# Transposes of queries, keys and attention output by DMA instead of by TensorE products, in an attention + MLP kernel

## The chip, the cores and the metric

One core of a Trainium2 chip. Times are device microseconds (us) of one execution. "Faster" and "slower" mean by over 2%. Executions that lie over 1.5% above the fastest of the same kernel count as slow; every ratio below is from fast executions alone. "Half clock" means that the profile records TensorE's granted clock at half of full speed. A bank is a piece of PSUM that holds one result.

## The reference, cut to what matters

Cosine attention for 8 batches of 12 heads, 448 positions and 64 elements; its output, with the heads side by side, is the input of a two-layer MLP.

```python
q_n = q / (norm(q, axis=-1) + 1e-6)            # q, k, v: (8, 12, 448, 64), fp32
k_n = k / (norm(k, axis=-1) + 1e-6)
attn = softmax(q_n @ k_n.T / tau)               # tau = 0.1
x = (attn @ v) with heads side by side          # (3584, 768)
h = x @ w_in                                    # (768, 2048)
out = (h * clip(h + 3, 0, 6) / 6) @ w_out       # (2048, 768)
```

## The kernel before

The kernel works on 48 pairs of heads. The first 18 pairs are run from a hand-written plan, in which every token is one step; pairs 18 to 47 are run by a loop. In iteration i the loop computes the scores and probabilities of pair i, finishes pair i - 1, prepares pair i + 2, and puts "units" of the MLP of the batch before (`UU`) between these, so that TensorE has work while other engines do theirs. Queries and keys are loaded with positions on partitions, but the score product reads them with the 64 elements of a head on partitions (`64*128 64x448` in the profile). So each normalised tile `nrm` (128 partitions, 7 slots, 2 heads of 64) is transposed by seven products with the identity, and the result is copied out of PSUM:

```python
def products(j, part):                      # "TM": one tile of queries or keys, in two parts
    t0, n = ((0, 4), (4, 3))[part]
    z, key = bank_of(None, readers(j, t0, n))
    for t in range(n):
        o = z[:, t * 128 : (t + 1) * 128]
        nc.tensor.matmul(o, nrm[:, slots(j)[t0 + t], :, :], ident[:, :], start=True, stop=True)

def copy_k(i, e="v", part=None):            # "CK": six slots of 64 keys, PSUM fp32 -> SBUF bf16
    ...
    copy(e, kz[i % 2][:, c0 + 64 * (a - odd) : c0 + 64 * (b - odd)], z[:, a - t0 : b - t0, x, :])

def copy_k3(i, e="v"):                      # "CS": the seventh slot, each half on its own partitions
    ...
    for g in range(2):
        p = slice(64 * g, 64 * g + 64)
        copy(e, kz[i % 2][p, c : c + SR], z[p, t : t + 1, x, :])      # 64 partitions x 64 elements

# the loop
for i in range(FIRST, NP):
    for g in range(3): do("SC", i, g)       # scores, then exponentials, then probabilities x values
    ...
    do("FI", i - 1); do("SC", i, 3); do("EX", i, 3)
    for part in range(2):
        prepare(("TM", i + 2, part))        # queries in even iterations, keys in odd ones
        if even:  prepare(("CQ", i + 2, "v", part), ("CQ", i + 3, "v", part))
        else:     ...                       # CK and CS of pairs i + 1 and i + 2
        if part == 0: do("UU", 1)
    prepare(("SQ", i + 5, "p", 0, 7))       # "p": GpSimd
    do("UU", n - 1)
    do("BK", i - 1); do("CX", i - 1, ...)   # attention output: 4 products, one copy from PSUM
    if not even: prepare(("NO", (i + 3) // 2))
    do("UU", n_u - n)
    prepare(("NM", i + 3, "p"), ("VC", i + 2, "p"), ("RE", i + 5), ("LQ", i + 7))
    if not even: prepare(("LV", (i + 5) // 2))
    do("VA", i, 0)
```

GpSimd computes squares (`SQ`), normalises (`NM`) and casts values (`VC`); VectorE has the copies, the MLP's product `gT` and the sums.

## Time and profile before

| | before |
|---|---|
| time, 3 runs | 456.58 us (451.35 to 458.17) |
| span of the profiled run | 452.1 us |
| TensorE busy | 432.4 us (96%), 3,891 matmuls |
| VectorE, ScalarE, GpSimd busy | 62%, 62%, 38% |
| load and store queue, share of 16 DMA engines | 37.9% |
| chain of work that ended last | 87% of the span on TensorE |

Busy shares are of the span. What counts is the last row: after the loads of the start, TensorE is never without work (idle for 0.04 us after 80 us), so the time is TensorE's list of work. The lines that show it are in the prediction. Two more groups matter later, the small key copies, which read PSUM in the kernel before, and the score products. In the groups, the columns are count, busy us, mean ns of one, and the idle time before them:

```profile
L317 DVE CAST kz<-M 64x64 bf16<-64x64 f32 x40 | 8.7, 217 | 0.5 <-PE M L306 0.2
L395 PE MATMUL M<-qT,kz 64*128 64x448 bf16 (+1 forms) x193 | 41.8, 353 | 1.1 <-DVE kz L359 0.5
```

### The profile page before, as it was taken

The page shows a single profiled execution, that of the slowest core. Times are in us where ns is not written, and L with a number is a line of the kernel's source. Part 1 is how long each engine was busy: PE and PEld are TensorE (multiplying, and loading weights), DVE is VectorE, ACT ScalarE, POOL GpSimd, SP SyncE. Part 2 cuts the span into 40 slices and gives each one's busy share as a digit, 9 for nine tenths or more (in the row PEclk, how much of TensorE's full clock was granted, in tenths as well). Part 3 has the DMA queues.
Part 4 walks back from the last instruction along what each step waited for, and adds up shares of the span by engine and source line. Part 5 has one row for each costly group of instructions (what it writes and reads, how often), then busy time and mean ns, then how long its engine had stood idle before and what let it go on. Part 6 is the DMA issues. An engine that isn't in the chain of part 4 may idle for free.

```text
span 452.1 us, 9918 instructions
## 1 busy us (share of the span) xinstructions
PE 432.4 (96%) x3891; PEld 259.8 (57%) x3891; DVE 279.1 (62%) x603; ACT 279.7 (62%) x625; POOL 172.0 (38%) x149
## 2 busy tenths in 40 slices
PE   4879799999999999999999999999999999999996
PEld 1446455556665666666666666666666665655563
DVE  6888688678566675576776675566776552304400
ACT  5769799986676755576576575567577565214410
POOL 4869479603007361542652551633641400000000
PEclk9669999999999999999999999999999999999999
DMA  7999999912252443435343444425432011121032
GB/s 218 276 226 263 252 233 215 233 24 79 68 146 78 125 136 85 123 79 145 107 128 95 110 106 131 122 60 137 128 83 65 19 32 40 36 70 36 0 72 70
DMA packets 39695, 52.55 MB, mean 116 GB/s; under 512 B 4320, under 2 KB 38112, under 8 KB 39648
## 3 DMA queue, kind: packets, MB, share of 16 engines
q1 hardware_dynamic: 35536, 45.07, 37.9%
q0 software_dynamic: 3712, 6.29, 7.8%
q8 instruction: 30, 0.49, 0.5%
q10 hardware_dynamic: 400, 0.56, 0.4%
q14 instruction: 17, 0.14, 0.1%
HBM read 47.19 MB, written 11.01 MB: 129 GB/s over the span
## 4 chain that ended last, share of the span: by engine, by line
PE 87%; DMA 7%; issue 2%; POOL 1%; SPq 1%; ACT 1%; DVE 0%; POOLq 0%; ACTq 0%
PE M L493 23%; PE M L527 21%; PE PV L437 10%; PE Z L493 7%; PE Y L527 6%; PE M L395 5%; PE Z L527 5%; DMA raw<-in_k_dram 3%; DMA w_in_sb<-in_moe_w_in_dram 3%; PE Y L493 2%; PE Z L395 2%; PE M L306 2%; PE M L474 1%; PE Y L306 1%; PE Y L395 1%
## 5 line engine op out<-in xcount | busy, mean ns | idle before, releaser
L527 PEld LDWEIGHTS <-gT 128*128 128x128 bf16 x896 | 86.8, 98 | 57.6 <-issue 0.2
L493 PE MATMUL M<-xT,w_in_sb 128*128 128x448 bf16 x546 | 115.3, 352 | 0.0
L250 POOL TENSOR_TENSOR nrm<-raw,r 128x896 bf16<-128x896 f32 (+1 forms) x44 | 74.6, 1697 | 102.4 <-ACT r L238 102.3
L412 ACT ACTIVATE at<-M 128x448 bf16<-128x448 f32 x193 | 93.7, 564 | 29.8 <-PE M L395 20.0
L493 PEld LDWEIGHTS <-w_in_sb 128*128 128x128 bf16 x768 | 70.5, 98 | 57.0 <-issue 4.5
L527 PE MATMUL M<-w_out_sb,gT 128*128 128x384 bf16 x592 | 101.0, 326 | 0.0
L207 POOL TENSOR_TENSOR sq<-raw 128x896 f32<-128x896 f32 (+7 forms) x46 | 67.0, 1458 | 70.2 <-DMA raw<-in_k_dram 28.9
L508 DVE SCALAR_TENSOR_TENSOR gT<-u,M 128x448 bf16<-128x448 bf16 x91 | 56.2, 620 | 32.4 <-ACT u L502 31.2
L502 ACT ACTIVATE u<-M,half_bias 128x448 bf16<-128x448 f32 x91 | 58.8, 649 | 23.5 <-PE M L493 22.8
L437 PEld LDWEIGHTS <-at 128*128 128x128 bf16 x1344 | 54.1, 99 | 24.9 <-issue 19.0
L437 PE MATMUL PV<-vx,at 128*128 128x65 bf16 (+1 forms) x1344 | 65.5, 200 | 0.0
L219 DVE TENSOR_REDUCE n<-sq 128x14 f32<-128x896 f32 (+1 forms) x50 | 51.8, 1040 | 2.4 <-POOL sq L207 1.5
L395 PE MATMUL M<-qT,kz 64*128 64x448 bf16 (+1 forms) x193 | 41.8, 353 | 1.1 <-DVE kz L359 0.5
L412 ACT ACTIVATE at<-Z 128x448 bf16<-128x448 f32 x56 | 31.6, 564 | 13.2 <-PE M L395 13.1
L544 DVE COPY o<-M 128x384 f32<-128x384 f32 x19 | 10.6, 557 | 42.5 <-PE M L527 42.5
L493 PE MATMUL Z<-xT,w_in_sb 128*128 128x448 bf16 x162 | 35.1, 352 | 0.0
L453 DVE TENSOR_TENSOR on<-PV,rc 128x512 bf16<-128x512 f32 x48 | 33.2, 692 | 1.7
L452 DVE RECIPROCAL rc<-PV 128x8 f32<-128x8 f32 x48 | 9.9, 206 | 37.8 <-PE PV L437 37.8
L542 ACT COPY o<-M 128x384 f32<-128x384 f32 x17 | 8.1, 478 | 38.6 <-PE M L527 38.6
L527 PE MATMUL Y<-w_out_sb,gT 128*128 128x384 bf16 x176 | 30.4, 326 | 0.0
L263 POOL CAST vx<-vr 128x512 bf16<-128x512 f32 x43 | 26.2, 614 | 10.9 <-DMA vr<-in_v_dram 10.9
L412 ACT ACTIVATE at<-Y 128x448 bf16<-128x448 f32 x45 | 25.3, 563 | 0.1
(91 smaller groups left out, 432.1 us busy)
## 6 DMA issues: line engine op xcount, KB each, us to landing
vr<-in_v_dram SPq DMA_DIRECT2D x96, 128.0 KB, 4.0
out_dram<-o SPq DMA_DIRECT2D x111, 96.0 KB, 2.2
raw<-in_q_dram SPq DMA_DIRECT2D x23, 448.0 KB, 5.3
raw<-in_k_dram SPq DMA_DIRECT2D x23, 448.0 KB, 4.0
w_in_sb<-in_moe_w_in_dram POOLq DMA_DIRECT2D x4, 768.0 KB, 12.5
w_out_sb<-in_moe_w_out_dram POOLq DMA_DIRECT2D x4, 768.0 KB, 11.1
raw<-in_q_dram SPq DMA_DIRECT2D x4, 112.0 KB, 3.4
raw<-in_k_dram ACTq DMA_DIRECT2D x4, 112.0 KB, 3.7
```

The costliest lines, as they stand in the source:

```text
L207: engines[e].tensor_tensor(out=o, in0=i, in1=i, op=ALU.mult)
L219: nc.vector.tensor_reduce(out=n2s[d % 2][:, j % 2, c], in_=sq[:, :, :, :].rearrange("p g c d -> p (g c) d")[:, c, :], axis=AX.X, op=ALU.add,)
L250: engines[e].tensor_tensor(out=nrm[:, :, g, :].rearrange("p c g d -> p g c d"), in0=raw_of[j][:, g, :, :], in1=rs[d % 2][3][:, j % 2, :] . ...
L263: engines[e].tensor_copy(out=vx[i % NVX][:, :, 0:D].rearrange("p (g c) d -> p g c d", g=2), in_=bass.AP(tensor=(t := vr[i // 2 % NV][:, i ...
L395: nc.tensor.matmul(o, kt[rows, c0 : c0 + 128], qt[rows, :], start=True, stop=True)
L412: nc.scalar.activation(out=o, in_=x, func=AF.Exp, scale=inv_tau)
L437: nc.tensor.matmul(o, at[:, n, q_cols(i // HP, j)], mv, start=(name == "A0" and j % 2 == 0), stop=last, skip_group_check=True,)
L453: nc.vector.tensor_tensor(out=on[:, :, :, :].rearrange("p (b j) h d -> p b (j h) d", b=2), in0=pv4[:, :, :, 0:D], in1=rc[:, :, :].to_broad ...
L493: nc.tensor.matmul(ps[:, 0:S], w_in_sb[:, cc, fc * 128 : (fc + 1) * 128], x[:, cc, :], start=(cc == 0), stop=(cc == CC - 1),)
L502: nc.scalar.activation(out=u[:, :], in_=ps[:, 0:S], func=AF.Relu, bias=half_bias[:, :], scale=1.0 / 6.0)
L508: nc.vector.scalar_tensor_tensor(out=g[:, fc, c0 : c0 + S], in0=u[:, :], scalar=1.0, in1=ps[:, 0:S], op0=ALU.min, op1=ALU.mult,)
L527: nc.tensor.matmul(ps[:, 0:MH], lhs, w_out_sb[:, fc, m * MH : (m + 1) * MH], start=(fc == 0), stop=(fc == FCN - 1),)
```

## The change

Its intent is to take the transposes off TensorE. From tile 14 on, `nrm` is transposed by one DMA, SBUF to SBUF (`XD`), and from pair 12 on the attention output too (`XB`), both on the sync queue. The score product reads queries straight from the transposed tile `tT`, so the query copies go. The key copies now read `tT` in SBUF. Positions keep their natural slot order. In the loop, the keys' copies move behind the second MLP unit.

```diff
+    def crossbar(j):
+        ...
+        nc.sync.dma_start_transpose(
+            out=tT[j % 4][:, :, :, :].rearrange("p c n e -> p c (n e)"),
+            in_=nrm[:, :, :, :].rearrange("p c g d -> p (c g d)"),
+        )
+    def back_crossbar(i):
+        ...
+        nc.sync.dma_start_transpose(
+            out=xT[b % 2][:, hp, :].rearrange("p (j n) -> p j n", j=4),
+            in_=on[:, :, :, :].rearrange("p j h d -> p (j h d)"),
+        )
     def copy_k(i, e="v"):
         ...
+        f = bass.AP(tensor=f.tensor, offset=f.offset, ap=[f.ap[0], [128, 3], [512, 2], [1, 64]])
+        nc.vector.tensor_copy(out=kz[i % 2][:, 0:KM].rearrange("p (j h e) -> p j h e", j=3, h=2), in_=f)
     def copy_k3(i, e="v"):
         ...
         for g in range(2):
             ...
             copy(e, kz[i % 2][p, c : c + SR], z[p, t : t + 1, x, :])   # z is now tT, in SBUF
     def scores(...):
         ...
+        kt, qt = kz[i % 2], tT[jq % 4][:, :, i % 2, :] if jq >= XJ else qT[i % 4]
     # the loop
-        for part in range(2):
-            prepare(("TM", i + 2, part))
-            ...
-            if part == 0:
-                do("UU", 1)
+        do("XB", i - 1)
+        prepare(("XD", i + 2))
+        do("UU", 1)
         prepare(("SQ", i + 5, "p", 0, 7))
         do("UU", n - 1)
-        do("BK", i - 1)
-        do("CX", i - 1, "a" if i % HP == 0 else "v")
+        if not even:
+            prepare(("CK", i + 1), ("CS", i + 1), ("CK", i + 2), ("CS", i + 2))
...
-    NV, NR = 3, 8
+    NV, NR = 3, 7
```

Cut: the same replacement in the plan (`TM`, `CQ`, `BK`, `CX` become `XD`, `XB`), slot order, fills of the pads, one buffer of `u` fewer (3, not 4), and the order of two units at a batch's start.

## The prediction

> **What bounds the kernel now.** I read first the page of the profile (busy shares, the slices, the chain that ended last), then the view of windows, then the timeline of one steady iteration, engine by engine. The slices:
>
> ```profile
> PE   4879799999999999999999999999999999999996
> ...
> POOL 4869479603007361542652551633641400000000
> PEclk9669999999999999999999999999999999999999
> DMA  7999999912252443435343444425432011121032
> ...
> PE 87%; DMA 7%; issue 2%; POOL 1%; SPq 1%; ACT 1%; DVE 0%; POOLq 0%; ACTq 0%
> ```
>
> The kernel has two stages. Until about 80 us the DMA rows are full (loads of queries, keys, values and weights) and TensorE is not. From 80 us on TensorE is busy in every slice, at the full granted clock, and the chain that ended last runs along it for 87% of the span. DMA is at 0.1 to 0.5 there. A busy TensorE need not be at its peak, so I look at one steady iteration in the timeline of TensorE (start, length, what):
>
> ```profile
> 242.44 0.35 PE L395 MATMUL M<-qT,kz 128*128 128x448 bf16 x1
> 242.63 0.39 PE L306 MATMUL Y<-ident,nrm 128*128 128x128 bf16 x4
> 242.90 1.29 PE L493 MATMUL Z<-xT,w_in_sb 128*128 128x448 bf16 x6
> 244.03 0.33 PE L306 MATMUL M<-ident,nrm 128*128 128x128 bf16 x3
> 244.19 1.30 PE L493 MATMUL M<-xT,w_in_sb 128*128 128x448 bf16 x6
> 245.33 0.36 PE L474 MATMUL M<-ident,on 128*128 128x128 bf16 x4
> 245.53 1.30 PE L493 MATMUL M<-xT,w_in_sb 128*128 128x448 bf16 x6
> 246.66 2.76 PE L527 MATMUL Y<-w_out_sb,gT 128*128 128x384 bf16 x16
> 249.26 0.41 PE L437 MATMUL PV<-vx,at 128*128 128x65 bf16 x8
> ```
>
> Each block starts as soon as the one before allows: six products of the first MLP matmul take 1.13 us (188 ns each), sixteen of the second 2.60 us (163 ns). There is no gap to win; only work can be taken off. The iteration lasts some 8.6 us, and in the windows of 20 us from 160 to 260 us VectorE is busy 12 to 14 us, ScalarE 11 to 13, GpSimd 8 to 11: none is near being the bound.
>
> [...] what such a product costs in a full pipeline: one record lasts 219 ns, while the next matmul starts 50 to 60 ns after it. I count by starts.[...] Nothing in the kernel before shows a DMA transpose[...].[...] in this iteration two stores issued at 241.4 and 242.0 move their 1,536-byte packets until about 244, and then the 1,792-byte packets of the load issued at 242.6 follow, to about 246.
>
> **The change, part by part.** *Taken from TensorE.* From the instruction lists: all 238 products of line 306 (queries and keys, 34 tiles of two heads by 7) and 144 of the 176 of line 474 (attention output, 36 head pairs by 4). From the timeline, per pair: 242.63 to 242.90 is 0.27 us, 244.03 to 244.19 0.16, 245.33 to 245.53 0.20. That is 34 x 0.43 + 36 x 0.20 = 21.8 us. Summed over the whole trace from each product's start to the next matmul's, line 306 costs 238 x 58.5 ns = 13.9 us and the removed part of line 474 144 x 50.4 ns = 7.3 us: 21.2 us, all after 80 us, all on the path. I use 21.2.
>
> *Taken from VectorE and ScalarE.* 61 query copies (30 of 349 ns, 31 of 415), 29 copies of attention output (618 ns) and 25 small copies on ScalarE go; the key copies read bf16 in SBUF, not fp32 in PSUM. That is over 40 us of VectorE and some 9 of ScalarE, beside the path: worth nothing by itself. Three PSUM banks fewer per pair are taken from the ring of six; TensorE did not wait for banks, so nothing either.
>
> *Added.* 34 DMA transposes of 128x896 bf16 (229 KB) and 36 of 128x512 (131 KB), 12.5 MB, all on the sync queue, which executes in order and already has loads and stores.[...] In 360 us that adds 35 GB/s to rows that are under half used: bandwidth is no bound. Latency is the question, in three places.
>
> (a) Odd iterations, 14 in the loop. There the keys' transpose is issued right behind the attention output's, and VectorE's key copies stand after the second MLP unit, ahead of the third unit's product. In the trace the last probability product of the pair before ends near 242.6, normalising on VectorE ends at 243.57, and the sync queue is free by 243.2. So the output's transpose goes out at 243.6. Issue: 0.6 us, what a load's issue takes[...] (a store takes 2.2 us from issue to landing, 0.55 of it issue)[...]. When is it needed? Without the removed products, the next scores start at 242.6 + 3 x 1.13 + 2.6 + 0.5 = 249.1, the third pair of them at 249.5, in the bank that the third unit's product has to free; that product (0.62) stands behind the key copies (about 1 us): the transpose has to land by 247.9. The estimate is 0.3 to 0.8 us late[...]. I take 0.35 us x 14 = 5 us.
>
> (b) Batch boundaries, five in the loop. The last pair's output is needed by the first unit of the next batch. The change puts a second-matmul unit ahead of it: two carried units and that one, 2.26 + 2.6 + 0.2 = 5.1 us after the last probability product. But the sync queue has a query load and four value loads ahead. The boundary near 288 us, where that product ends at 288.4:
>
> ```profile
> 288.50 0.59 SPq L176 DMA_DIRECT2D raw<-in_q_dram  x1
> 289.20 2.64 SPq L191 DMA_DIRECT2D vr<-in_v_dram  x4
> ```
>
> So the output's transpose is issued from 291.85, 3.4 us after the product, with 960 KB ahead in the rings;[...] some 0.8 us late. 5 x 0.8 = 4 us.
>
> (c) The planned part before pair 18, and the start: one raw buffer fewer (7, not 8) makes loads wait for one normalisation more, 1 to 2 us each while DMA is the bound; 8 small fills more on GpSimd. I take 1 us.
>
> Sum: 21.2 - 5 - 4 - 1 = 11 us less. The two runs before that are within 1.5% of the fastest have a mean of 454, so 443; I lean a little to the better side, 442, as the change moves the key copies and the units just where a transpose of this latency would land.
>
> **The rivals.** *All hidden.* The copies of (a) come in time and (b) overlaps: 454 - 21 = 433. For it: TensorE is the only bound and DMA has over half its time free. Against it: the in-order queue of (b). *The issue becomes the wait.* If a DMA transpose holds the sync queue or the rings twice as long as I assume, the keys land some 3 us later, and 14 odd iterations lose 3 us each, 42 us against 21: some 470.[...] For it: no run here shows a transpose's cost.[...] *VectorE held at its queue's head.* The key copies wait, and the products behind them free no bank; the same as (a), but also where TensorE has slack. It would show as 440 to 450. *The scores slow down* because queries are read in runs of 64 elements, not in one: 330 products; the keys' side is unchanged, and I see nothing for it; 10% more would be 3 us.
>
> **Range and chances.** Hidden (433) and issue-bound (470) are the ends; half the weight lies between 434 and 446. Range 428 to 460. Faster by over 2% means under 445: 0.60. Within 2%: 0.26. Slower: 0.14.
>
> **What would show it right or wrong.** Right: the steady iteration at 8.0 to 8.3 us, not 8.6; lines for the products of queries and keys gone; TensorE with idle time of 0.3 to 1 us before scores in odd iterations put down to the key copies, and these to the keys' DMA transpose; about 1 us before the first MLP unit of a batch put down to the output's transpose; a transpose of 229 KB landing 3.5 to 4.5 us after its issue begins. Wrong, to the good: no such waits, 433. Wrong, to the bad: transposes landing after 6 us or more, the sync queue's issue time over 6 us per iteration, and VectorE waiting for DMA several us in each odd iteration. If the start is longer than 80 us by several us, (c) was mis-sized.

How long a transpose would take to issue and to land, and with it the 5 and 4 us of (a) and (b), was my guess: no trace of the kernel before shows a DMA transpose.

## The result, and the profile after

| | before | after |
|---|---|---|
| time, 4 runs each | 455.55 us (451.35 to 458.17) | 532.04 us (531.1 to 534.81) |
| ratio, 95% interval | | 1.1733 (1.1658 to 1.1809), slower |
| matmuls | 3,891 | 3,509 |
| TensorE busy | 96% | 85% |

A ratio is the mean time of one kernel's fast runs over that of the other's of the same rounds, so it is not quite the ratio of the medians. The four runs after are fast; of the four before, the one of 458.17 us is 1.5% above the fastest and counts as slow. All results are correct. The forecast of 442 us was wrong: the kernel became 17% slower. The rows of the slices and the chain that ended last, kernel after:

```profile
PE   4788999679979798876969678897976989999996
PEclk9988999798979989989779797998978889999999
DMA  8999899643474464654656445473743322223013
PE 48%; DMA 21%; DVE 15%; SPq 6%; issue 5%; ACT 2%; POOL 2%; POOLq 0%; DVEq 0%; ACTq 0%
```

TensorE has holes all along (6 to 8 where there were 9s), its granted clock has holes as well, and only 48% of the chain lie on it. VectorE, with 0% of the chain before, has 15%. DMA is still far from full: its share between 80 and 444 us is 0.52, against 0.34 between 80 and 440 us before.

Summing the trace from each matmul's start to the next one's, and setting apart the gaps after a matmul's modelled end, gives an account of TensorE's time (us):

| | before | after | difference |
|---|---|---|---|
| the transposing products | 32.2 | 11.0 | -21.2 |
| all other matmuls, same count | 399.9 | 437.7 | +38 |
| idle | 12.9 | 73.7 | +61 |
| of that, idle ahead of scores | 3.5 | 56.0 | +52 |
| time at half clock | 21.0 | 83.6 | +63 |

So the work did go off TensorE, to the tenth of a us. What came instead are waits ahead of the scores, and other matmuls that take longer. The half clock goes with the latter: of the 63 us more at half clock TensorE was idle in about 10, and half of the rest, an estimated 27 us, is lost work, most of the 38: at half clock the products of the first MLP matmul start 373 ns apart in the median, at full clock 189. The trace's clock records after have 16 stretches at half clock, of 3.4 or 6.8 us but for the last (1.7 us, at the end); all the others begin in a wait of TensorE or within 1.2 us of the end of one.

One odd iteration shows the mechanism. TensorE, kernel after (start, length, what, idle before and what ended it):

```profile
288.65 2.76 PE L537 MATMUL Z<-w_out_sb,gT 128*128 128x384 bf16 x16
291.25 0.41 PE L440 MATMUL PV<-vx,at 128*128 128x65 bf16 x8
291.59 0.55 PE L401 MATMUL M<-tT,kz 64*128 64x448 bf16 x4
296.29 0.53 PE L401 MATMUL Y<-tT,kz 64*128 64x448 bf16 x1 [4.15 <-DVE gT L518]
```

After four score products TensorE waits 4.15 us for `gT`, the MLP product of VectorE that frees the bank for the third pair of scores. The score product after the wait takes 0.53 us, not 0.35: a stretch at half clock began at 294.4. What did VectorE do meanwhile?

```profile
291.02 0.35 DVE L357 COPY kz<-tT 128x384 bf16<-128x384 bf16 x1 [2.02 <-DMA tT<-nrm]
291.29 2.10 DVE L320 COPY kz<-tT 64x64 bf16<-64x64 bf16 x2
293.40 0.35 DVE L357 COPY kz<-tT 128x384 bf16<-128x384 bf16 x1
293.67 1.92 DVE L320 COPY kz<-tT 64x64 bf16<-64x64 bf16 x2
295.62 0.62 DVE L518 SCALAR_TENSOR_TENSOR gT<-u,Y 128x448 bf16<-128x448 bf16 x1
```

It waited 2 us for the keys' transpose (foreseen, though not that long). Then two copies of 64 x 64 elements took 2.1 us and two more 1.9 us, while a copy of 128 x 384 elements, twelve times as many, took 0.35. And GpSimd in that stretch:

```profile
291.10 0.61 POOL L270 CAST vx<-vr 128x512 bf16<-128x512 f32 x1
291.67 1.68 POOL L214 TENSOR_TENSOR sq<-raw 128x896 f32<-128x896 f32 x1
293.31 1.69 POOL L257 TENSOR_TENSOR nrm<-raw,r 128x896 bf16<-128x896 f32 x1
294.94 0.61 POOL L270 CAST vx<-vr 128x512 bf16<-128x512 f32 x1
```

The first two small copies end at 293.39, just after GpSimd's instruction of 291.67 ends (293.35). The last end at 295.59, just after its cast ends (295.55). Over the whole trace, 47 of the 68 small copies took over 180 ns; every one of these began beside a GpSimd instruction and ended 30 to 37 ns after one ended. The other 21 took 162 to 179 ns. As a group, kernel after (this line and the next are the counterparts of the small copies and of the scores before):

```profile
L320 DVE COPY kz<-tT 64x64 bf16<-64x64 bf16 x68 | 50.5, 742 | 11.1 <-DMA tT<-nrm 10.6
L401 PE MATMUL M<-tT,kz 64*128 64x448 bf16 (+1 forms) x193 | 48.8, 380 | 30.8 <-DVE gT L518 18.1
```

742 ns each against 217 before, when they read PSUM. The view of waits lists TensorE's and VectorE's waits (us in total, times, longest):

```profile
DVE kz L357 <- DMA tT<-nrm: 25.5, 13, 3.5
...
PE M L401 <- DVE gT L518: 18.1, 9, 4.2
...
PE Y L401 <- DVE gT L518: 15.4, 5, 4.2
...
DVE kz L320 <- DMA tT<-nrm: 10.6, 3, 5.7
```

VectorE waits 36 us in 16 places for keys' transposes, so landing is a second suspect beside the copies. The transposes themselves, from the page's list of DMA issues (count, median us from issue to landing), are not slow beside a load of 448 KB, 4.7 and 4.8 us in the same list; their 12.5 MB took 71 us of 16 engines' time, some 176 GB/s, in packets of 256 bytes of 18 ns in the median:

```profile
xT<-on SPq DMA_TRANSPOSE x36, 3.3
tT<-nrm SPq DMA_TRANSPOSE x34, 2.8
```

**My theory** (P in the expectations) is that the small copies, which now have source and destination in SBUF, wait for GpSimd's instructions to end: the 47 that took over 180 ns, up to 1,662, ended 30 to 37 ns after one did. They stand ahead of `gT`, which stands ahead of the scores, and a hole of TensorE goes with half clock (15 of the 16 stretches above). Not every copy inside SBUF is held. The trace records the small copy as 64 elements on both sides, the large one as 3 blocks in the source and one run of 384 in the destination: 162 to 1,662 ns for the one, 342 to 354 ns for all 34 of the other, though 25 of these began beside a GpSimd instruction. So SBUF on both sides is not enough; what inside the chip makes the small one wait, no trace shows. That another operation on the same bytes, a maximum over one element, is not held was a guess, which e1 tests. Below, "plain" names the small copy as the change has it, "maximum" its other spelling.

**Rivals.** (1) (L in the expectations) The DMA transposes land late, and the copies only show it; then moving the transposes earlier, or the keys back to TensorE, is what helps. (2) The sync queue or the added traffic is the limit. (3) The copies are long for their shape alone (64 partitions), GpSimd or not.

### The profile page after: what moved, and what is told of

The parts are those of the page before. It is cut to its first block, busy times and chain, and to the rows that moved or that the text cites. A ratio compares the mean times of both kernels' runs of the same rounds, so it can differ in the third digit from the quotient of the medians.

```text
span 529.6 us, 9158 instructions
## 1 busy us (share of the span) xinstructions
PE 449.0 (85%) x3509; PEld 252.3 (48%) x3509; DVE 274.8 (52%) x492; ACT 277.7 (52%) x600; POOL 172.5 (33%) x157
## 4 chain that ended last, share of the span: by engine, by line
PE 48%; DMA 21%; DVE 15%; SPq 6%; issue 5%; ACT 2%; POOL 2%; POOLq 0%; DVEq 0%; ACTq 0%
PE M L503 13%; PE M L537 11%; DMA tT<-nrm 11%; DVE kz L320 7%; PE PV L440 7%; PE M L401 4%; PE Z L503 3%; PE Y L537 3%; PE Y L503 3%; SPq L487 3%; DVE gT L518 3%; PE Z L537 2%; DMA xT<-on 2%; DMA w_in_sb<-in_moe_w_in_dram 2%; DMA raw<-in_q_dram 2%
## 5 line engine op out<-in xcount | busy, mean ns | idle before, releaser
L503 PEld LDWEIGHTS <-w_in_sb 128*128 128x128 bf16 x768 | 79.1, 105 | 79.7 <-issue 25.1
L440 PEld LDWEIGHTS <-at 128*128 128x128 bf16 x1344 | 60.6, 105 | 56.8 <-issue 50.1
L440 PE MATMUL PV<-vx,at 128*128 128x65 bf16 (+1 forms) x1344 | 72.8, 210 | 3.4 <-DVE on L456 2.9
L401 PE MATMUL M<-tT,kz 64*128 64x448 bf16 (+1 forms) x193 | 48.8, 380 | 30.8 <-DVE gT L518 18.1
L320 DVE COPY kz<-tT 64x64 bf16<-64x64 bf16 x68 | 50.5, 742 | 11.1 <-DMA tT<-nrm 10.6
L401 PEld LDWEIGHTS <-kz 64*128 64x128 bf16 (+1 forms) x330 | 17.4, 97 | 57.8 <-issue 43.2
L419 ACT ACTIVATE at<-Y 128x448 bf16<-128x448 f32 x53 | 29.4, 555 | 27.2 <-PE Y L401 14.3
L401 PE MATMUL Y<-tT,kz 64*128 64x448 bf16 (+1 forms) x53 | 20.2, 381 | 18.7 <-DVE gT L518 15.4
L537 PE MATMUL Z<-w_out_sb,gT 128*128 128x384 bf16 x192 | 33.2, 326 | 0.0
L503 PE MATMUL Z<-xT,w_in_sb 128*128 128x448 bf16 x126 | 31.0, 387 | 0.0
```

The source lines that it names most:

```text
L320: nc.vector.tensor_copy(out=out, in_=in_)
L401: nc.tensor.matmul(o, kt[rows, c0 : c0 + 128], qt[rows], start=True, stop=True)
L419: nc.scalar.activation(out=o, in_=x, func=AF.Exp, scale=inv_tau)
L440: nc.tensor.matmul(o, at[:, n, q_cols(i // HP, j)], mv, start=(name == "A0" and j % 2 == 0), stop=last, skip_group_check=True,)
L503: nc.tensor.matmul(ps[:, 0:S], w_in_sb[:, cc, fc * 128 : (fc + 1) * 128], x[:, cc, 0:S], start=(cc == 0), stop=(cc == CC - 1),)
L537: nc.tensor.matmul(ps[:, 0:MH], lhs, w_out_sb[:, fc, m * MH : (m + 1) * MH], start=(fc == 0), stop=(fc == FCN - 1),)
```

## The experiments

Twelve kernels ran, all with correct results. Ratios are to the kernel before in the same rounds; its medians were 453.69 us (beside e1 to e4), 452.73 (e5 to e8) and 452.42 (e9 to e12).

### e1: the small copies as a maximum (after the theory)

Against the kernel after; the maximum over one element is a copy.

```diff
-            copy(e, kz[i % 2][p, c : c + SR], z[p, t : t + 1, x, :])
+            if key is None:
+                nc.vector.tensor_reduce(out=kz[i % 2][p, c : c + SR],
+                    in_=z[p, t : t + 1, x, :].rearrange("p t (n o) -> p (t n) o", o=1), axis=AX.X, op=ALU.max)
+            else:
+                copy(e, kz[i % 2][p, c : c + SR], z[p, t : t + 1, x, :])
```

> The 64x64 key copies of the changed kernel (68, from SBUF to SBUF on VectorE) are written as a maximum over one element: same engine, same bytes, same place in the order[...]. Theory P (the long copies, 742 ns mean and up to 1.64 us where GpSimd is at work[...]; they hold up the product behind them, which frees a bank, and TensorE stands still for some 4 us in each odd iteration and comes back at half clock): copies about 200 ns everywhere, idle time of TensorE before scores falls from 56 us to under 25, half-clock time well under the 83 us of before, the whole at 460 to 480 us. Rival L (the wait is for the keys' transposes to land, the copies only fill time that VectorE would have waited): copies short, waits of the key copies for the transpose as before (36 us), the whole over 515 us.

Measured: 474.58 us (473.18 to 477.88), ratio 1.0449 (1.0384 to 1.0514). 57 us are gone by another spelling of 68 small copies, as theory and range had it; the rival's "over 515 us" did not come. The copies (least, median, most ns), kernel e1:

```profile
L369 DVE TENSOR_REDUCE kz<-tT x68: 200/214/218, 90.0 to 394.3; 64x64 bf16<-64x64 bf16 x68
```

and in the kernel after:

```profile
L320 DVE COPY kz<-tT x68: 162/544/1662, 93.8 to 447.7; 64x64 bf16<-64x64 bf16 x68
```

The maximum is slower at its best (200 against 162 ns), but never held up (218 ns at most), though 54 of the 68 began beside a GpSimd instruction. The wait for the keys' transposes stayed, 26.7 us in 14 places against 25.5 in 13. Idle ahead of scores fell from 56.0 to 23.9 us and time at half clock from 83.6 to 48.5. The kernel is still 4.5% slower than before, so a second cause is there.

### e2: keys' transposes issued earlier, copies as they are

Against the kernel after; the transpose of keys goes out at the head of the odd iteration.

```diff
     for i in range(FIRST, NP):
+        if not even:
+            prepare(("XD", i + 2))
         ...
-        prepare(("XD", i + 2))
+        if even:
+            prepare(("XD", i + 2))
```

> Copies as in the changed kernel, but the keys' transpose is issued at the head of the odd iteration, ahead of the attention output's. Theory P: the wait of the key copies for the transpose goes (36 us in all to near 0), but copies still wait for GpSimd at other moments; the time falls by less than a third of what is lost, 505 to 525 us. Rival L: TensorE's waits vanish and the time is under 470 us.

Measured: 514.09 us, ratio 1.1345 (1.1272 to 1.1417), inside the range. But the edit did not do what was expected of it: the key copies' wait for the transposes fell from 36 us to 27, not to near 0. Issued at the head of the iteration, most of the loop's keys land 4.2 to 6.0 us after their issue begins, not 2.6 to 4.4. So the earlier issue brings 18 us of the 77, and rival 1 is weakened, not removed, by this run; what refutes it as the main cause are e1 and e5.

### e3: both of these edits

> Both[...]. Theory P plus the landing wait as a second, smaller part: 440 to 455 us, with only the batch boundaries (output transposes behind the value loads) left as TensorE waits, some 5 x 2 us. If a third cause is at work, for instance slower scores from queries in 64-element runs or DMA contention, it stays above 470.

Measured: 470.56 us, ratio 1.0402 (1.0318 to 1.0487). The expected 440 to 455 us were missed. Against e1 the intervals overlap, so this earlier issue adds little once the copies are free; but here too the wait in the loop only fell, from 26.7 us in 14 places to 18.5 in 9. Another part of what is left sits where the edit does not reach, in the planned part. There the sync queue itself is held by a transpose, among loads (in the kernel after, where two such issues take 4.4 and 5.3 us, the DMA share is 1.06 from 80 to 100 us), kernel e3 (the second column is the length of the issue, in the first line of two):

```profile
74.31 5.87 SPq L309 DMA_TRANSPOSE tT<-nrm  x2
...
82.05 5.16 SPq L309 DMA_TRANSPOSE tT<-nrm  x1
```

and VectorE, then TensorE, wait for what it brings:

```profile
88.27 0.44 DVE L369 TENSOR_REDUCE kz<-tT 64x64 bf16<-64x64 bf16 x2 [5.68 <-DMA tT<-nrm]
```
```profile
89.68 0.36 PE L409 MATMUL Y<-tT,kz 64*128 64x448 bf16 x1 [2.22 <-DVE kz L357]
```

Elsewhere an issue takes 1.2 us in the median. Of the 25.7 us for which TensorE is idle after 80 us in e3, 11.4 lie between 80 and 150 us: 3.9 behind these key copies, 3.8 for the output at the first batch boundary, the rest in two waits for VectorE. The other 14.3 us are in the loop.

### e4: keys back on TensorE, queries and output by DMA

Against the kernel after (and `TR.15`, `TR.17`, `TR.19` in place of `XD` in the plan); the keys are again read from PSUM.

```diff
-        if j >= XJ:
+        if j >= XJ and j % 2 == 0:
...
-        prepare(("XD", i + 2))
+        prepare(("XD" if even else "TR", i + 2))
```

> Keys again by TensorE transposes into PSUM from pair 14 on, queries and attention output still by DMA. Key copies then read PSUM[...]. Theory P and rival L both foresee most of the loss gone: 17 x 7 transposes at some 58 ns = 7 us more on TensorE than the full change, 14 us less than the kernel before; with boundary waits some 440 to 455 us. Over 500 us would mean that neither names the cause.

Measured: 452.01 us, ratio 0.996 (0.99 to 1.0019): same as before. Without key copies inside SBUF and without a key transpose to wait for, idle ahead of scores is 5.1 us and time at half clock 25.9. Its 76 small key copies, bf16 from PSUM, took 170 to 195 ns, and none of the 31 that began beside a GpSimd instruction was held; so it is the source in SBUF, not bf16, that goes with the long copies. So the keys carried the loss. The gain of what is still off TensorE is nearly all eaten at the batch boundaries, kernel e4, the sync queue and then TensorE:

```profile
131.43 0.49 SPq L183 DMA_DIRECT2D raw<-in_q_dram  x1
132.02 1.21 SPq L487 DMA_TRANSPOSE xT<-on  x1
```
```profile
137.05 0.53 PE L503 MATMUL Z<-xT,w_in_sb 128*128 128x448 bf16 x1 [3.93 <-DMA xT<-on]
```

The output's transpose stands behind a load of 448 KB and lands 5.0 us after its issue begins. Three of the other four boundaries wait 0.7 to 1.1 us.

### e5 and e6: the kernel before with useless small copies added, plain and as a maximum

Four copies of 64 x 64 elements of a constant tile at the end of each odd iteration (the change has the key copies somewhat earlier, ahead of the third unit); nothing waits for them but what stands behind them on VectorE. No DMA transpose is in these kernels.

```diff
+        if not even and i + 2 < NP:
+            for x in range(4):
+                p = slice(64 * (x % 2), 64 * (x % 2) + 64)
+                nc.vector.tensor_copy(out=extra[p, 64 * x : 64 * x + 64], in_=ident[p, 0:64])   # e5
+                # e6: nc.vector.tensor_reduce(..., in_=ident[p, 0:64] as (n o), axis=AX.X, op=ALU.max)
```

> The kernel before, with no DMA transpose at all, and four copies of 64x64 bf16 from SBUF to SBUF (an unused tile) on VectorE added in each of 14 odd iterations, at the end of the iteration where GpSimd squares and normalises. Theory P: the copies last 1 to 1.6 us each where GpSimd is busy, some 56 of them cost VectorE 40 us or more, and as VectorE stands still for some 3 us per odd iteration the time grows by 10 to 40 us. Rival L: 180 ns each, 0.7 us per iteration off the path, no change.

> The control of the run before: the same four copies at the same place, written as a maximum over one element[...]. Both theories: about 210 ns each, within 1% of the kernel before. If it too is slower by several per cent, the place in VectorE's order is what costs[...].

Measured: e5 478.35 us, ratio 1.0572 (1.0508 to 1.0635); e6 454.24 us, ratio 1.003 (1.0005 to 1.0054). The copies of e5, then of e6:

```profile
L715 DVE COPY extra<-ident x56: 164/541/1637, 145.9 to 398.0; 64x64 bf16<-64x64 bf16 x56
```
```profile
L715 DVE TENSOR_REDUCE extra<-ident x56: 199/215/218, 146.7 to 372.2; 64x64 bf16<-64x64 bf16 x56
```

This separates the cause cleanly. The same 56 copies of the same data, as plain copies, cost 25 us in a kernel without any DMA transpose; as a maximum, about 1 us. In e5 all 39 copies that began beside a GpSimd instruction ended 29 to 37 ns after that ended, and the other 17 took 164 to 179 ns. Rival 3 falls (same shape, same partitions), and rivals 1 and 2 are not present here. What TensorE waited for is another product than in the change: 21.6 us in 12 places, for VectorE's `on` ahead of the output's transposing products. Time at half clock was 24.3 us, hardly more than before, so the copies cost time without it too.

### e7: keys on TensorE, loads behind the transposes

e4, with the loads of an iteration issued after its transpose instead of ahead of it, and the output of the last planned pairs on TensorE again.

```diff
-            do("XB", i - 1)                      # e4
+        do("XB", i - 1)                          # pair 17: BK and CX
         prepare(("XD" if even else "TR", i + 2))
+        prepare(("LQ", i + 6))
+        if even and i > FIRST:
+            prepare(("LV", (i + 4) // 2))
...
-        prepare(("NM", i + 3, "p"), ("VC", i + 2, "p"), ("RE", i + 5), ("LQ", i + 7))
-        if not even:
-            prepare(("LV", (i + 5) // 2))
+        prepare(("NM", i + 3, "p"), ("VC", i + 2, "p"), ("RE", i + 5))
```

> Queries from the eighth pair on and attention output from pair 18 on by DMA; keys, and output before pair 18, by TensorE; loads of queries and keys and of values are issued behind the iteration's transposes, not ahead of them. If the remaining waits of the run with keys on TensorE (3.9 us and half a clock at the first batch boundary, 0.7 to 1.1 us plus 0.5 at four later ones) come from transposes that queue behind loads, they vanish: TensorE's work is 21 - 7 - 1 = 13 us less than before, time 438 to 446 us. If they stay, the queue order was not their cause: 448 to 453.

Measured: 446.13 us, ratio 0.9862 (0.9815 to 0.9909), 1.4% less than before, which is "same" by the 2% rule, at the upper end of the expected 438 to 446. No wait for the output's transpose is left in the trace.

### e8: keys by DMA an iteration ahead, small copies as a maximum

e7, but with the keys' transpose in the loop back on DMA. Keys are normalised one iteration sooner and go out right behind the queries in the even iteration, a whole iteration before the copies; the small copies are a maximum, as in e1. In the plan the keys of tiles 15, 17 and 19 stay on TensorE.

```diff
+    do("NM", FIRST + 3, "p")                     # ahead of the loop
...
-        prepare(("XD" if even else "TR", i + 2))
+        if even:
+            prepare(("XD", i + 2), ("XD", i + 3))
...
-        prepare(("NM", i + 3, "p"), ("VC", i + 2, "p"), ("RE", i + 5))
+        if not even:
+            prepare(("NM", i + 3, "p"), ("NM", i + 4, "p"))
+        prepare(("VC", i + 2, "p"), ("RE", i + 5))
```

The expectation takes three things for the loss: the held copies, the landing of the keys and the loads ahead of the output.

> All three by DMA in the loop (keys before pair 20 and output before pair 18 by TensorE)[...], keys normalised and transposed one iteration earlier (a full iteration ahead of their copies), loads behind transposes. [...]TensorE's idle time after 80 us is under 5 us and half-clock time as in the kernel before: some 20 us less TensorE work, 432 to 440 us. If TensorE still waits in odd iterations, there is a fourth cause: over 445.

Measured: 438.92 us (437.27 to 441.36), ratio 0.9699 (0.9652 to 0.9746): faster than both kernels, and inside the range. Slices and chain, kernel e8:

```profile
PE   4779999999999999999999999999999999999995
...
PEclk9679999999999999999999999999999999999999
...
PE 86%; DVE 5%; DMA 4%; ACT 2%; POOL 1%; issue 0%; SPq 0%; ACTq 0%; POOLq 0%
```

TensorE is full again at full clock, idle for 3.8 us after 80 us. Its steady iteration, from the first MLP block of one to that of the next:

```profile
251.37 1.30 PE L511 MATMUL M<-xT,w_in_sb 128*128 128x448 bf16 x6
...
254.78 2.76 PE L545 MATMUL M<-w_out_sb,gT 128*128 128x384 bf16 x16
...
259.39 0.92 PE L511 MATMUL M<-xT,w_in_sb 128*128 128x448 bf16 x4
```

8.0 us, against 8.6 before.

### e9: e8 with plain copies

> The best version so far (keys ahead, loads behind, planned part on TensorE), but the 64x64 key copies are plain copies again, as in the changed kernel. Theory P: with the transposes long landed[...]: copies of 0.5 to 1.6 us where GpSimd works, TensorE waits of 1 to 4 us in most odd iterations and half clock after the long ones; 20 to 50 us more, 460 to 490 us. If GpSimd happens to be idle at the copies in this order, the cost is small, and the copies are about 170 ns: the trace tells which.

Measured: 470.72 us, ratio 1.0384 (1.0319 to 1.0449). The profiled run was over 1.5% above the fastest, so I take no times of stretches from it. Transposes far ahead and loads behind them do not help where copies are held: by the ratios, 31 us separate e9 from e8, which differ in the spelling of 56 copies.

### e10: e8 with loads ahead of the transposes

The loads go back to their old place, all else as in e8.

> The best version, but with the loads of queries, keys and values issued where the changed kernel issues them, ahead of the next iteration's transposes. The four later batch boundaries should each lose 0.7 to 1.2 us again, as in the run with keys on TensorE: 3 to 6 us more, 442 to 445 us. No difference would mean that the order of loads and transposes on the queue does not matter.

Measured: 442.71 us, ratio 0.979 (0.9732 to 0.9849), unclear by the 2% rule. By the medians the order on the sync queue is worth 3.8 us, but the two intervals touch (e8's ends at 0.9746); the trace agrees with it: the waits for the output's transpose are back, 0.66 to 1.98 us at three boundaries.

### e11: the small copies on ScalarE

Against the kernel after: the 64 x 64 copies go to ScalarE.

```diff
-            copy(e, kz[i % 2][p, c : c + SR], z[p, t : t + 1, x, :])
+            copy("a" if key is None else e, kz[i % 2][p, c : c + SR], z[p, t : t + 1, x, :])
```

> The changed kernel, its 64x64 key copies on ScalarE[...]. [...]about as fast[...] (475 us), within 10 us either way, copies 200 to 250 ns; ScalarE then waits for the keys' transpose at the head of its own queue, so a little slower is possible.[...]

Measured: 496.41 us, ratio 1.0966 (1.0912 to 1.1019). 36 us better than after, so the copies' engine matters, but 22 us worse than e1, more than I expected. The copies take 240 to 247 ns; only 3 of the 68 began beside a GpSimd instruction, so that they were not held says little. ScalarE now waits for the keys' transposes at the head of its queue, 41.4 us in 17 places, and holds exponentials and MLP work behind it. The copies were mended, and the landing wait about doubled: 69 us with VectorE's 27.5, against 36.

### e12: the output back on TensorE, keys and queries as in the change

The loop and the plan again transpose the attention output by products (`BK`, `CX`).

> The changed kernel with the attention output back on TensorE, queries and keys by DMA, key copies as changed. If the keys' copies are the main loss, this is still far slower than the kernel before, 505 to 530 us: TensorE gets 7 us of work back, the boundary waits (some 7 us) and the output's share of the queue go. Under 480 would mean that the output's transposes were the main loss.

Measured: 517.2 us, ratio 1.1421 (1.1346 to 1.1497). Without the output's transposes the kernel is 15 us better, although 7 us of products came back; whether the queue or the boundaries brought that, this run does not separate. The small copies still have a median of 545 ns and go up to 1,700, so the large loss stays.

## Why the prediction was wrong

Two steps failed outright, and one of them is by far the largest; (a) and (c) were mis-sized. They are taken in the order of the prediction.

**What is removed: right.** 21.2 us predicted, 21.2 measured, and all of it on the path: in e8, where nothing new waits, the steady iteration has the predicted 8.0 to 8.3 us.

**"the key copies read bf16 in SBUF, not fp32 in PSUM" and "worth nothing by itself": this is the step that failed.** I counted the six key copies of an odd iteration (two large, four small) as "about 1 us" and took a copy inside SBUF to be no dearer than one from PSUM. With their source in SBUF, the 64 x 64 copies wait for GpSimd: 742 ns in the mean, not 217, and the six take 4.6 us in the iteration shown. Their place ahead of the third unit's product made this 2 to 4 us of TensorE's waiting in most odd iterations. Size: 57 us of the 77 (after against e1), 31 us where everything else is mended (e9 against e8), 24 us in the kernel before (e5 against e6). Why the sizes differ is not shown; the slack ahead of what waits may differ. That it is the meeting with GpSimd is shown by the ends of the copies (30 to 37 ns after those of GpSimd's instructions, in e5 29 to 37) and by e5 and e6. What inside the chip does it is not shown.

**A wait costs what it lasts: failed, unspoken.** The prediction added up waits as if TensorE came back at full speed. It often comes back at half clock for 3.4 or 6.8 us. In the kernel after this is an estimated 27 us on top of 61 us of idle time. It explains why the loss is larger than the waits in any list. I did not vary a wait's length by itself, but the traces have waits of many lengths. In those of fast profiled runs, counting waits after 80 us that began at full clock, a stretch at half clock began in the wait or within 3.5 us of its end for all 34 waits over 3 us, for 20 of 23 between 2 and 3 us and for 14 of 38 between 1 and 2 us (3 of 18 where no other wait was near).

**(a) Keys landing late, 5 us: right mechanism, too small.** VectorE waited 25.5 us in 13 places on the large key copies, all in the loop, and 10.6 on the small ones, in the plan. The cost to TensorE by itself is read in e1, where the copies are not held: 12 us of waits in the loop behind the key copies (without those of 0.47 us that e8 has too), not 5. The transposes were better than feared: an issue took 1.2 us in the median, for 131 KB as for 229 KB, and a landing 2.8 us in the median, not 3.5 to 4.5. In the kernel after, the loop's keys landed 5.1 to 7.5 us after the last probability product began, where the prediction had 5.6 to 6.1 after its end. What was too small is again the price of the copies: unheld, two of 0.35 and four of 0.21 us (e1) are 1.5 us, not 1. With that the prediction's own sum gives an estimated 0.85 us x 14 = 12 us. The closeness may be luck, as the landings spread widely. With the held copies the same wait stood on one path: the earlier issue, which took away a third of the loop's wait, brought 18 us with plain copies (e2) and no clear gain with the maximum (e3 against e1).

**(b) Batch boundaries, 4 us: about right.** TensorE waited 5.2 us in three places for the output in the kernel after; in e4 3.93 us at the first boundary and 0.7 to 1.1 us at three others; some 3.8 us by the order on the queue (e10 against e8).

**(c) The planned part, 1 us: too small.** I looked there for one buffer and eight fills. What happened is that the transposes of that part came among loads (DMA share 1.06 from 80 to 100 us in the kernel after), with issues of up to 5.3 us and landings up to 12 us. VectorE begins pair 17's `on`, just behind the planned part, at 135.6 us in e3 and at 127.6 in e8, whose plan leaves these keys and outputs on TensorE: 8 us. That this part is better left on TensorE is supported by e7 and e8, which do so; neither tested that alone.

**The rivals of the prediction.** "The issue becomes the wait" is refuted for the loop by issues of 1.2 us. "VectorE held at its queue's head" was the nearest, but I tied it to landing alone and put it at 440 to 450. ("The issue becomes the wait" was also added up wrongly: 42 us of loss against 21 of gain on 454 is 475, not 470.) "The scores slow down" from 64-element runs is refuted: score products take 353 ns in the mean in e8 and in the kernel before; the 380 of the kernel after come with its half clock. "All hidden", 433, was in reach: e8 gets within 6 us of it with 45 of the transposing products left in the plan.

**What stays open.** The exact share of (a) in the 77 us, since the parts are not a sum; what the planned part costs when it alone is changed; what inside the chip makes a plain small copy wait for GpSimd; and from what length on a wait is followed by half clock, as no run varied that alone (in e1 a stretch of 6.8 us began 0.2 us after a wait of 2.15). One observation of the kernel after that no run tested: of 87 packets of transposes that took over 700 ns, 74 were in flight together with a fetch of instructions (packets of 16 KB).

## What to carry to other kernels

Before moving a copy's source from PSUM to SBUF, look at what GpSimd does at that time: here a small VectorE copy with source and destination in SBUF lasted until GpSimd's instruction ended (up to 1,662 ns, not 162), and another form of it (a maximum over one element) was safer though slower at its best (200 ns, 218 at most). When an operation moves to DMA, ask where its consumer stands in its engine's order, and not only for its bandwidth: e8 issues it a whole iteration ahead of that consumer and ahead of the loads on the same queue, and no copy waits for it. And price a TensorE wait of over 2 us above its length: here 54 of 57 such waits were followed by half clock.
